# Writing the transposed K in another order, replacing a cross-partition maximum, and visiting later code first: one decode-attention kernel

## The chip, the cores and the metric

One core of a Trainium2 chip. The metric is the device time of one execution in microseconds (us). Some executions fall into a slower state (in experiment 1 two took 116.31 and 115.04 us at a mean granted clock of 0.87 and 0.85, against 113.21 and 112.99 us at 0.92 and 0.89), and these are left out of every comparison here. PE is the matmul engine, DVE the vector engine, ACT the scalar engine, POOL and SP the other two; SP only issues transfers here. The "granted clock" is the share of its full clock that PE was given. "Landing" is the moment at which a transfer has signalled its end.

## The reference, cut to what matters

```python
xn = layernorm(x)                                   # x: 2 x 1 x 448
q  = (xn @ wq)                                      # 16 query heads of 256
k, v = last 2048 rows of the caches, 8 kv heads, each for 2 query heads
s  = softmax(q k^T / 16) v @ wo
g  = silu(relu(xn @ w1) @ w2)
out = x + s * g
```

K and V of two batch entries and eight heads are 33.6 MB, and the weights bring the total to 44 MB. All of it is read once.

## The kernel before

Work goes in four units u = 0..3 (one batch entry, four heads each). T stands for the transposes of K, S for the score matmuls, PV for the matmuls of the softmax weights with V. The 2048 rows of a head are spread over 32 row groups r, and partition p of `kbuf` holds row group r and head h as p = 4 r + h. DVE transposes K in blocks of 32x32 (32-bit elements, each a pair of bf16 values), and PE multiplies the result with the queries. Four matmuls, one for each head, run side by side in four column strips of the array (in the trace of the kernel before one score matmul lasts 1.07 us, and eight of them take 1.97 to 2.00 us together).

```python
def do_T(u, blk):                       # DVE: 2048 elements of 32 bits per partition
    src = kbuf[u % 2][:, :].bitcast(F32).tensor
    dst = kt[blk][:, :].bitcast(F32).tensor
    ... e.transpose(view(dst, 0, [[1, 32 * NT]]), view(src, 32 * blk, [[DH // 2, NT], [1, 32]]))
        # waits for K of u and for the scores of u - 1 that read kt[blk]

def do_S(u, blk):                       # PE: eight matmuls
    for par in range(2):
        for i in range(4):              # head i
            ... mm(sbk[32 * i:32 * i + 8, :], qz[:, lo:lo + 8], view(kt[blk], 2 * i + par, [[64, NT], [8, 8]]), ...,
                   tile_position=(0, 32 * i))
```

A row of a transposed block holds its 32 columns in the order of the partitions, j = 4 r' + h (r' = 0..7). One head therefore takes every fourth 32-bit element: a step of 8 bf16 values, 16 bytes.

The softmax needs, for every score row, a bias that is the maximum over several partitions. Before, it goes through PE twice:

```python
rm   = max over the columns of sbk                       # DVE, 128 x 1
mbk  = transpose of rm by matmul with an identity         # PE
mrow = grouped max, negated, on one partition             # DVE
mall = mrow spread over 128 columns                       # DVE
mbk  = mall^T @ one                                       # PE: back to 128 partitions
bias = copy of mbk                                        # DVE
```

Transfers are issued from one queue in this order: wq (first part), K0, wq (rest), K1, V0, w1, w2; then K2 and V1 when T of u = 0 and the q matmuls are done; K3 after T of u = 1; V2 after PV of u = 0; V3 in two parts after PV of u = 1; wo in seven parts, shrinking in size, last. The end of the kernel is PV of u = 3, a few small steps, and 128 small matmuls with wo.

Of the kernel before, what the change touches and what calls it, by code (L numbers as in the profile page):

```python
# [22 lines left out]
class _Prog:  # L23
# [13 lines left out]
        self.lists[eng].append(o)  # L37
        return o

    def run(self, block):  # L40
        n = 0
        for ops in self.lists.values():
            for o in ops:
                for d in o.deps:
                    d.needed = True
        for e, ops in self.lists.items():
            sem, count = self.es.enter_context(self.nc.semaphore(f"s_{e}")), 0
            for o in ops:
                if o.dma:
                    n += 1  # L50
                    o.sem, o.value = self.es.enter_context(self.nc.semaphore(f"d_{n}")), 16
                elif o.needed:
                    count += 1
                    o.sem, o.value = sem, count

        def emit(eng, ops):
            seen = {}
            for o in ops:
                want = {}
                for d in o.deps:  # L60
                    if d.value > want.get(id(d.sem), (None, 0))[1]:
                        want[id(d.sem)] = (d.sem, d.value)
                for key, (sem, value) in want.items():
                    if value > seen.get(key, 0):
                        eng.wait_ge(sem, value)
                        seen[key] = value
                made = o.fn(eng) if o.fn else None
                if o.needed:
                    made.then_inc(o.sem, 16 if o.dma else 1)

        for name, e in (("gpsimd", POOL), ("sync", SP), ("scalar", ACTE), ("vector", DVE), ("tensor", PE)):
            def body(eng, ops=self.lists[e]):
                emit(eng, ops)
            getattr(block, name)(body)


def bass_recurrent_scan__sliding_block_cached__dense_activation_relu__decode_kernel(
# [27 lines left out]
    FC = DFF // 2  # L105
    WO_PARTS = [9, 7, 5, 4, 3, 2, 2]
    NWO = 16
    FIRST = 2
    NCOL = D // 4
    NROW = 4 * B  # L110
# [2 lines left out]
    with es:  # L113
        pr = _Prog(nc, es)

        def named(name, shape, dt):
            return es.enter_context(nc.sbuf_tensor(name, shape, dt))
# [4 lines left out]
        def view(t, off, dims, n=128, p0=0, pstep=1):  # L122
            width = t.shape[1]
            return bass.AP(t, p0 * width + off, [[width * pstep, n]] + dims)

        ident = named("ident", [128, 128], BF)
        ident_f = named("ident_f", [128, 128], F32)
        one_f = named("one_f", [128, 1], F32)
        par8 = named("par8", [128, 8], F32)
        par2 = named("par2", [128, 2], F32)  # L130
        qmask = named("qmask", [128, 8], F32)
# [23 lines left out]
        tmp = named("tmp", [NROW, NCOL], F32)  # L155
        out_sb = named("out_sb", [NROW, NCOL], BF)
        rm = named("rm", [128, 1], F32)
        mrow = named("mrow", [128, 8], F32)
        mall = named("mall", [128, 128], F32)
        bias = named("bias", [128, 1], F32)  # L160
        et = named("et", [128, 1024], BF)
        e_sb, e_t = et[:, 0:512], et[:, 512:1024]
# [44 lines left out]
        def load_v(u, cuts=(0, NT)):  # L207
# [15 lines left out]
        p_id = pr.op(POOL, lambda e: e.affine_select(  # L223
            out=ident[:, :], in_=ident[:, :], compare_op=ALU.not_equal, fill=1.0,
            base=0, pattern=[[-1, 128]], channel_multiplier=1), [i0])
        i1 = pr.op(POOL, lambda e: e.memset(ident_f[:, :], 0.0), [p_id])
        p_idf = pr.op(POOL, lambda e: e.affine_select(
            out=ident_f[:, :], in_=ident_f[:, :], compare_op=ALU.not_equal, fill=1.0,
            base=0, pattern=[[-1, 128]], channel_multiplier=1), [i1])
        p_one = pr.op(POOL, lambda e: e.memset(one_f[:, :], 1.0), [p_idf])  # L230
        p_z = [pr.op(POOL, lambda e, t=t: e.memset(t[:, :], 0.0)) for t in (mall, qrep, spread, h_z, at_z)][-1]

        a_z = [pr.op(ACTE, lambda e, t=t: e.memzero(t[:, :])) for t in (obk, sbk, hbk, obk_last)][-1]

# [7 lines left out]
        for e2 in range(2):  # L242
# [6 lines left out]
            out=par2[:, :], in_=view(ident, 0, [[1, 2], [2, 64]]), axis=AX.X, op=ALU.add), [p_id])  # L249
        v_par8 = pr.op(DVE, lambda e: e.tensor_copy(  # L250
            view(par8, 0, [[2, 4], [1, 2]]), view(par2, 0, [[0, 4], [1, 2]])), [v_par])
        v_qm = pr.op(DVE, lambda e: e.tensor_reduce(
            out=qmask[:, :], in_=view(ident, 0, [[16, 8], [1, 16]]), axis=AX.X, op=ALU.add))

# [34 lines left out]
        def do_T(u, blk):  # L289
            src = kbuf[u % 2][:, :].bitcast(F32).tensor  # L290
            dst = kt[blk][:, :].bitcast(F32).tensor
            st["T", u] = st["kt", u, blk] = pr.op(DVE, lambda e: e.transpose(  # L292
                view(dst, 0, [[1, 32 * NT]]), view(src, 32 * blk, [[DH // 2, NT], [1, 32]])),
                [d_k[u], st.get(("S", u - 1, blk))])

        def do_S(u, blk):
            b, v = divmod(u, 2)
            deps = [st["q"], st["kt", u, blk], st.get(("exp", u - 1)), a_z]
            for par in range(2):
                for i in range(4):  # L300
                    lo = 64 * (4 * i + 2 * v + b) + 8 * (2 * blk + par)
                    o = pr.op(PE, mm(sbk[32 * i:32 * i + 8, :], qz[:, lo:lo + 8], view(kt[blk], 2 * i + par, [[64, NT], [8, 8]]),
                                     blk == 0 and par == 0, blk == NBLK - 1 and par == 1, tile_position=(0, 32 * i)), deps)
                    deps = []
            st["S", u, blk] = o

        def softmax(u, fill=()):
            fill = list(fill)

            def meanwhile():  # L310
                if fill:
                    fill.pop(0)()

            meanwhile()
            v = pr.op(DVE, lambda e: e.tensor_reduce(out=rm[:, :], in_=sbk[:, :], axis=AX.X, op=ALU.max),  # L315
                      [st["S", u, NBLK - 1], st.get(("rmT", u - 1))])
            m = st["rmT", u] = pr.op(PE, lambda e: e.matmul(
                mbk_ap(0, 128, 1), lhsT=rm[:, :], rhs=ident_f[:, :], start=True, stop=True,
                is_transpose=True), [v, p_idf, st["mbk"]])
            v = pr.op(DVE, lambda e: e.tensor_reduce(  # L320
                out=view(mrow, 0, [[2, 4], [1, 2]], n=1), in_=view(mbk, 0, [[32, 4], [1, 2], [2, 4]], n=1), axis=AX.X, op=ALU.max, negate=True),
                [m])
            meanwhile()
            v = pr.op(DVE, lambda e: e.tensor_copy(  # L324
                view(mall, 0, [[32, 4], [2, 4], [1, 2]], n=1), view(mrow, 0, [[2, 4], [0, 4], [1, 2]], n=1)),
                [v, p_z, st.get(("bias", u - 1))])
            m = st["bias", u] = pr.op(PE, mm(mbk_ap(128, 1), mall[0:1, :], one_f[0:1, :], True, True), [v, p_one])
            v = st["mbk"] = pr.op(DVE, lambda e: e.tensor_copy(bias[:, :], mbk_ap(128, 1)),  # L328
                                  [m, st.get(("exp", u - 1))])
            meanwhile()  # L330
            a = st["exp", u] = pr.op(ACTE, lambda e: e.activation(  # L331
                e_sb, sbk[:, :], ACT.Exp, bias=bias[:, 0:1], accum_out=ssum[:, 0:1]),
                [v, st.get(("e_t", u - 1)), st.get(("gs", u - 1))])
            v = st["e_t", u] = pr.op(DVE, lambda e: e.transpose(e_t, e_sb), [a, st.get(("Pt", u - 1))])  # L334
            deps = [v, v_sp, st.get(("pt", u - 1))]
            for x in range(4):
                for g in range(4):
                    lo = 128 * (4 * x + g)
                    o = pr.op(PE, mm(view(pbk, 2 * x, [[8, 16], [1, 2]]), spread[:, lo:lo + 128],
                                     view(et, 512 + 2 * g, [[32, 16], [1, 2]]), g == 0, g == 3), deps)  # L340
                    deps = []
            st["Pt", u] = o
            v = st["pt", u] = pr.op(DVE, lambda e: e.tensor_tensor(  # L343
                out=view(pt[u % 2], 0, [[8, NT], [2, 4], [1, 2]]), in0=view(pbk, 0, [[2, NT], [0, 4], [1, 2]]),
                in1=view(hmask, 0, [[0, NT], [1, 4], [0, 2]]), op=ALU.mult), [o, v_hm, st.get(("PV", u - 2))])
            meanwhile()
            m = st["gs", u] = pr.op(PE, mm(mbk_ap(130, 1), gsum[:, :], ssum[:, 0:1], True, True), [v_gs, a, st["mbk"]])
            st["rs", u] = st["mbk"] = pr.op(DVE, lambda e: e.reciprocal(rs[:, u:u + 1], mbk_ap(130, 1)), [m])
            assert not fill
# [122 lines left out]
        softmax(0)  # L472
        scores(1)
        load_k(3)
        softmax(1, [fill(0, (0,)), fill(), fill(0, (1, 2)), fill(0, (3,))])
        attend_scale(0)
        do_H()
        do_F()
        load_v(2)
        scores(2)  # L480
        softmax(2, [fill(1, (0,)), fill(), fill(1, (1, 2)), fill(1, (3,))])
        attend_scale(1)
        load_v(3, (0, 48, 64))
        d_wo, j0 = {}, 0
# [2 lines left out]
            d_wo[j0] = pr.dma(SP, wo_sb[:, j0 * D:(j0 + n) * D], wo_src[v, :, j * D:(j + n) * D], [st["T", 2]])  # L487
            j0 += n
        scores(3)
        softmax(3, [fill(2, (0,)), fill(n=1), fill(2, (1, 2), 2), fill(2, (3,), 2)])  # L490
        attend_scale(2)
        idle_work(6)
        do_PV(3, (0, 1))
        attend_turn(2)
        do_PV(3, (2,))
# [20 lines left out]
        pr.op(ACTE, None, [d_o])  # L516

        with nc.Block() as block:
            pr.run(block)


# [26 lines left out]
```

## Time and profile before

| | before |
|---|---|
| time, median of 4 runs | 113.56 us (113.40 to 116.04; the last is a slow one, and the median of the other three is 113.44) |
| span of the profiled run | 112.5 us |
| data read | 44.1 MB, 392 GB/s over the span |
| K transposes on DVE | 16 x 2.28 us |
| eight score matmuls | 1.97 to 2.00 us |
| softmax bias, from end of the maximum to the exponential | 1.4 us |
| last landing of wo (issue plus time to landing) | 107.6 us |
| end of the last matmul | 110.3 us |

A row of the table of groups has: line of the kernel, engine, operation, output <- inputs, partitions x elements, count | busy us in all, mean ns of one | idle us of the engine ahead of it, and what ended most of it.

```profile
L274 PE MATMUL sbk<-kt,qz 128*8 128x512 bf16 x128 | 31.0, 1070 | 14.2 <-DVE kt L292 12.0
L292 DVE STREAM_TRANSPOSE kt<-kbuf 128x2048 f32<-128x2048 f32 x16 | 35.9, 2283 | 4.8 <-DMA kbuf<-in_A_k_cache_dram 4.8
...
L274 PE MATMUL obk<-vbuf,pt 128*16 128x512 bf16 x96 | 7.2, 402 | 0.0
L274 PE MATMUL obk<-kbuf,at_z 128*8 128x112 bf16 x128 | 6.6, 213 | 0.0
```

The score matmuls and the PV matmuls have the same number of columns and the same four strips, yet one score matmul takes 1070 ns and one PV matmul 402. The wo matmuls (last line) had no idle time ahead of them: when PE came to them, wo was there.

The chain of waits, in order of time (start us, us, what), for the stretch of u = 1 and for the end:

```profile
40.59 8.80 DVE kt L292 x4
...
49.43 2.00 PE sbk L274 x8
...
51.45 0.70 DVE rm L315
...
52.20 0.28 PE mbk L317
...
52.51 0.19 DVE mrow L320
...
52.72 0.18 DVE mall L324
...
52.95 0.39 PE mbk L274 x2
...
53.36 0.17 DVE bias L328
...
53.55 0.79 ACT et L331 x2
...
102.05 0.57 PE obk_last L274 x8
...
104.70 5.62 PE obk L274 x112
```

Four transposes take 8.80 us, 2.20 each, and only the last block of score matmuls (2.00 us) lies on the chain, since the others hide behind the next transpose. In u = 2 and u = 3 one more block of eight (1.97 us) lies on it.

The table of stretches (stretch, length, then busy us and count for PE, PE weight load, DVE, ACT, POOL; granted PE clock with 1.00 for full speed, share of the 16 transfer engines, GB/s):

```profile
85.00:90.00 5.00, 4.49 (x29) 0.50 (x21) 4.93 (x5) 0.00 (x0) 0.00 (x0) 0.57 0.98 416
90.00:95.00 5.00, 4.07 (x27) 0.56 (x20) 2.36 (x4) 0.00 (x0) 0.00 (x0) 1.00 0.98 418
...
105.00:110.00 5.00, 5.00 (x106) 5.00 (x104) 0.00 (x0) 0.00 (x0) 0.00 (x0) 1.00 0.18 63
```

The transfer engines are full to the end of the data, as in every stretch from 5 us on, and PE still works 2.7 us after the last landing.

### The profile page before, as it was taken

Reading aid. Unit: us, or ns where it says so; the run is one execution under the profiler, and the core shown is the slowest. Engines: PE = TensorE matmul, PEld = TensorE weight load, DVE = VectorE, ACT = ScalarE, POOL = GpSimd, SP = SyncE. Lnnn points to the kernel's source line nnn. Section 1 sums busy time; section 2 is a strip of 40 time slices with the busy share of each in tenths; the row PEclk is TensorE's granted clock in tenths of the full one; section 3 lists DMA queues with packets and bytes.
Section 4 is the critical chain, followed back from the end, with each engine's and each line's share of the span. In section 5 each row is a group of like instructions: output and inputs, shape, how many; then the busy total and the mean of one; then the engine's idle time right before and its main releaser. Section 6 shows DMA issues by size and latency. Waiting matters only on the chain.

```text
span 112.5 us, 1423 instructions
## 1 busy us (share of the span) xinstructions
PE 65.0 (58%) x621; PEld 22.8 (20%) x621; DVE 61.3 (55%) x86; ACT 9.7 (9%) x18; POOL 3.8 (3%) x14
## 2 busy tenths in 40 slices
PE   0010000371996227997786329887509887898992
PEld 0000000110110220002346301012301002343991
DVE  2067059987002489954452499924699944425001
ACT  4980000000000200000200000002000000200000
POOL 6700000000000000000000000000000000000000
PEclk9999999999599755599859965699965699999999
DMA  3989989989989989998999999999899999999600
GB/s 68 493 373 524 408 386 429 489 373 501 431 373 489 443 339 400 511 444 373 454 466 387 419 472 396 419 477 408 384 483 396 402 428 399 430 405 407 225 6 1
DMA packets 3050, 44.20 MB, mean 393 GB/s; under 512 B 354, under 2 KB 612, under 8 KB 1508
## 3 DMA queue, kind: packets, MB, share of 16 engines
q1 hardware_dynamic: 3008, 44.11, 92.6%
q8 instruction: 5, 0.08, 0.3%
q10 hardware_dynamic: 36, 0.01, 0.0%
q14 instruction: 1, 0.01, 0.0%
HBM read 44.11 MB, written 0.00 MB: 392 GB/s over the span
## 4 chain that ended last, share of the span: by engine, by line
PE 40%; DVE 35%; DMA 17%; ACT 3%; issue 2%; SPq 1%
DVE kt L292 20%; DMA vbuf<-in_A_wq_dram 17%; PE sbk L274 15%; PE obk L274 10%; PE mbk L274 3%; ACT et L331 3%; PE pbk L274 3%; PE fbk L274 3%; DVE et L334 3%; DVE rm L315 2%; PE obk_last L274 2%; PE wbk L274 2%; PE hbk L274 1%; DVE o_sb L368 1%; DVE qz L408 1%
## 5 line engine op out<-in xcount | busy, mean ns | idle before, releaser
L274 PE MATMUL sbk<-kt,qz 128*8 128x512 bf16 x128 | 31.0, 1070 | 14.2 <-DVE kt L292 12.0
L292 DVE STREAM_TRANSPOSE kt<-kbuf 128x2048 f32<-128x2048 f32 x16 | 35.9, 2283 | 4.8 <-DMA kbuf<-in_A_k_cache_dram 4.8
L274 PE MATMUL obk<-vbuf,xr 128*4 128x512 bf16 x28 | 3.1, 618 | 13.2 <-DMA vbuf<-in_A_wq_dram 13.2
L315 DVE TENSOR_REDUCE rm<-sbk 128x1 f32<-128x512 f32 x4 | 2.8, 692 | 13.7 <-PE sbk L274 13.7
L331 ACT ACTIVATE et<-sbk,bias 128x512 bf16<-128x512 f32 x4 | 2.7, 687 | 76.2 <-DVE bias L328 76.2
L274 PEld LDWEIGHTS sbk<-kt,qz 128*8 128x8 bf16 x128 | 2.1, 87 | 29.2 <-DVE kt L292 21.9
L274 PE MATMUL obk<-vbuf,pt 128*16 128x512 bf16 x96 | 7.2, 402 | 0.0
L274 PE MATMUL obk<-kbuf,at_z 128*8 128x112 bf16 x128 | 6.6, 213 | 0.0
L274 PEld LDWEIGHTS obk<-kbuf,at_z 128*8 128x8 bf16 x128 | 6.3, 87 | 0.0
L274 PE MATMUL mbk<-ident,xg 2*128 2x2 bf16 x7 | 0.3, 163 | 8.0 <-DVE xg L243 8.0
L274 PE MATMUL pbk<-et,spread 128*128 128x32 bf16 x64 | 2.6, 193 | 3.8 <-DVE et L334 3.8
L334 DVE STREAM_TRANSPOSE et<-et 128x512 bf16<-128x512 bf16 x4 | 2.8, 712 | 3.4 <-ACT et L331 3.4
L343 DVE TENSOR_TENSOR pt<-pbk,hmask 128x512 bf16<-128x512 f32 x4 | 2.8, 692 | 3.0 <-PE pbk L274 3.0
L274 PEld LDWEIGHTS obk<-vbuf,xr 128*4 128x4 bf16 x28 | 0.8, 114 | 14.7 <-issue 14.7
L274 PE MATMUL fbk<-wf,h_z 128*8 128x112 bf16 x56 | 2.9, 213 | 1.4 <-DVE h_z L423 1.4
L274 PE MATMUL wbk<-q_n,ident 128*128 128x512 bf16 x13 | 3.6, 381 | 0.0
L274 PEld LDWEIGHTS pbk<-et,spread 128*128 128x128 bf16 x64 | 2.2, 104 | 5.4 <-DVE et L334 5.4
L511 DVE TENSOR_TENSOR tmp<-obk,g_sb 8x112 f32<-8x112 f32 x1 | 0.3, 263 | 5.4 <-PE obk L274 5.4
L274 PEld LDWEIGHTS fbk<-wf,h_z 128*8 128x8 bf16 x56 | 2.8, 87 | 1.8 <-issue 1.8
L274 PEld LDWEIGHTS obk<-vbuf,pt 128*16 128x16 bf16 x96 | 2.0, 92 | 5.6 <-issue 4.7
L274 PE MATMUL mbk<-one_f,mall 1*128 1x1 f32 x8 | 1.5, 256 | 1.7 <-DVE mall L324 1.7
L382 DVE TENSOR_TENSOR at_exp<-mbk,qmask 128x128 bf16<-128x128 f32 x4 | 1.2, 292 | 2.1 <-PE mbk L274 2.0
(76 smaller groups left out, 45.4 us busy)
## 6 DMA issues: line engine op xcount, KB each, us to landing
kbuf<-in_A_k_cache_dram SPq DMA_DIRECT2D x4, 4096.0 KB, 29.2
vbuf<-in_A_v_cache_dram SPq DMA_DIRECT2D x3, 4096.0 KB, 37.8
wf<-in_B_w_dram SPq DMA_DIRECT2D x2, 1568.0 KB, 43.8
vbuf<-in_A_v_cache_dram SPq DMA_DIRECT2D x1, 3072.0 KB, 15.3
vbuf<-in_A_wq_dram SPq DMA_DIRECT2D x1, 2560.0 KB, 19.6
vbuf<-in_A_wq_dram SPq DMA_DIRECT2D x1, 1024.0 KB, 4.9
vbuf<-in_A_v_cache_dram SPq DMA_DIRECT2D x1, 1024.0 KB, 17.2
kbuf<-in_A_wo_dram SPq DMA_DIRECT2D x1, 1008.0 KB, 19.0
```

The source lines that it names most:

```text
L274: return lambda e: e.matmul(out_ap, lhsT=lhsT, rhs=rhs, start=start, stop=stop, skip_group_check=True, **kw)
L292: st["T", u] = st["kt", u, blk] = pr.op(DVE, lambda e: e.transpose(view(dst, 0, [[1, 32 * NT]]), view(src, 32 * blk, [[DH // 2, NT], [1, 3 ...
L315: v = pr.op(DVE, lambda e: e.tensor_reduce(out=rm[:, :], in_=sbk[:, :], axis=AX.X, op=ALU.max), [st["S", u, NBLK - 1], st.get(("rmT", u - ...
L331: a = st["exp", u] = pr.op(ACTE, lambda e: e.activation(e_sb, sbk[:, :], ACT.Exp, bias=bias[:, 0:1], accum_out=ssum[:, 0:1]), [v, st.get(( ...
L334: v = st["e_t", u] = pr.op(DVE, lambda e: e.transpose(e_t, e_sb), [a, st.get(("Pt", u - 1))])
L343: v = st["pt", u] = pr.op(DVE, lambda e: e.tensor_tensor(out=view(pt[u % 2], 0, [[8, NT], [2, 4], [1, 2]]), in0=view(pbk, 0, [[2, NT], [0, ...
L368: v = st["osb", u] = pr.op(DVE, lambda e: e.tensor_scalar(out=o_sb[:, :], in0=view(out_bank(u), 0, [[1, 512]]), scalar1=rs[:, u:u + 1], sc ...
L382: st["at", u] = st["mbk"] = pr.op(DVE, lambda e: e.tensor_tensor(out=view(at_exp, 0, [[16, 8], [8, 2], [1, 8]]), in0=view(mbk, 136, [[1, 8 ...
L408: st["q"] = pr.op(DVE, lambda e, r=r: e.tensor_tensor(out=view(qz, r, [[64, 16], [8, 8], [2, 4]]), in0=view(q_t, 256 * r, [[1, 16], [32, 8 ...
L511: v_t = pr.op(DVE, lambda e: e.tensor_tensor(out=tmp[:, :], in0=obk[0:NROW, 0:NCOL], in1=g_sb[:, :], op=ALU.mult), [m_o, st["g"]])
```

## The change

The intent: let the score matmuls read `kt` at a step of 4 bytes instead of 16, by having the transpose write each block in the order h, r' instead of r', h; find the bias on DVE alone; and have PE jump, before anything else, to two later places of its own program and back, so that their instructions are fetched early (the trace of the changed kernel has four instruction fetches of 16 KB before 17 us, that of the kernel before none). There are also more idle matmuls, whose result nobody reads, ahead of the last PV.

```diff
@@ do_T
-                view(dst, 0, [[1, 32 * NT]]), view(src, 32 * blk, [[DH // 2, NT], [1, 32]])),
+                view(dst, 0, [[32, NT], [1, 8], [8, 4]]), view(src, 32 * blk, [[DH // 2, NT], [1, 32]])),
@@ do_S
-  view(kt[blk], 2 * i + par, [[64, NT], [8, 8]])
+  view(kt[blk], 16 * i + par, [[64, NT], [2, 8]])
@@ softmax: mbk, mrow, mall, mbk, bias (two on PE, three on DVE) become
+            v = pr.op(DVE, lambda e: e.transpose(rmt[:, :], view(rm, 0, [[0, 32]])), [v])
+            v = pr.op(DVE, lambda e: e.tensor_tensor(out=m8[:, :], in0=rmt[:, 0:8], in1=nmask[:, :], op=ALU.add), [v])
+            v = pr.op(DVE, lambda e: e.tensor_reduce(out=bias[:, :], in_=m8[:, :], axis=AX.X, op=ALU.max, negate=True),
+                      [v, st.get(("exp", u - 1))])
@@ emitting the PE program, with VISITS = [285, 530] (places among its operations)
+            if stubs:
+                nc.br("visit_0", engines=[eng.engine])
+                ...
+                if i in stubs:
+                    nc.br(f"past_{k}", engines=[eng.engine])
+                    nc.switch_bb(f"visit_{k}", parent=top)
+                    eng.nop()
+                    nc.br(next visit, or back to the start)
@@ (cut: set-up of nmask, unused identity tiles removed, fills regrouped)
-        idle_work(6)
+        idle_work(10)
```

The write pattern `[[32, 64], [1, 8], [8, 4]]` puts four elements 32 bytes (8 elements) apart, then starts again 4 bytes further on.

More of the change, by code (lines that the diff above doesn't have):

```diff
@@ L38, in dma, with run @@
         return o
-    def run(self, block):
-        n = 0
+    def run(self, block, stubs):
+        n, nc = 0, self.nc
         for ops in self.lists.values():
@@ L54, in run, with emit @@
                     o.sem, o.value = sem, count
-        def emit(eng, ops):
+        def emit(eng, ops, stubs=()):
             seen = {}
-            for o in ops:
+            if stubs:
+                nc.br("visit_0", engines=[eng.engine])
+                top = nc.cur_bb.parent
+                nc.switch_bb("visit_end", parent=top)
+            for i, o in enumerate(ops):
+                if i in stubs:
+                    k = stubs.index(i)
+                    nc.br(f"past_{k}", engines=[eng.engine])
+                    nc.switch_bb(f"visit_{k}", parent=top)
+                    eng.nop()
+                    nc.br(f"visit_{k + 1}" if k + 1 < len(stubs) else "visit_end", engines=[eng.engine])
+                    nc.switch_bb(f"past_{k}", parent=top)
                 want = {}
@@ L71, in run, with body @@
         for name, e in (("gpsimd", POOL), ("sync", SP), ("scalar", ACTE), ("vector", DVE), ("tensor", PE)):
-            def body(eng, ops=self.lists[e]):
-                emit(eng, ops)
+            def body(eng, ops=self.lists[e], e=e):
+                emit(eng, ops, stubs if e == PE else ())
             getattr(block, name)(body)
@@ L107, in bass_recurrent_scan__sliding_block_cached__dense_activation_relu__decode_kernel @@
     NWO = 16
+    VISITS = [285, 530]
     FIRST = 2
@@ L126, in bass_recurrent_scan__sliding_block_cached__dense_activation_relu__decode_kernel @@
         ident = named("ident", [128, 128], BF)
-        ident_f = named("ident_f", [128, 128], F32)
-        one_f = named("one_f", [128, 1], F32)
         par8 = named("par8", [128, 8], F32)
@@ L157, in bass_recurrent_scan__sliding_block_cached__dense_activation_relu__decode_kernel @@
         rm = named("rm", [128, 1], F32)
-        mrow = named("mrow", [128, 8], F32)
-        mall = named("mall", [128, 128], F32)
+        nmask = named("nmask", [128, 8], F32)
+        rmt = named("rmt", [128, 32], F32)
+        m8 = named("m8", [128, 8], F32)
         bias = named("bias", [128, 1], F32)
@@ L225, in bass_recurrent_scan__sliding_block_cached__dense_activation_relu__decode_kernel @@
             base=0, pattern=[[-1, 128]], channel_multiplier=1), [i0])
-        i1 = pr.op(POOL, lambda e: e.memset(ident_f[:, :], 0.0), [p_id])
-        p_idf = pr.op(POOL, lambda e: e.affine_select(
-            out=ident_f[:, :], in_=ident_f[:, :], compare_op=ALU.not_equal, fill=1.0,
-            base=0, pattern=[[-1, 128]], channel_multiplier=1), [i1])
-        p_one = pr.op(POOL, lambda e: e.memset(one_f[:, :], 1.0), [p_idf])
-        p_z = [pr.op(POOL, lambda e, t=t: e.memset(t[:, :], 0.0)) for t in (mall, qrep, spread, h_z, at_z)][-1]
+        p_z = [pr.op(POOL, lambda e, t=t: e.memset(t[:, :], 0.0)) for t in (qrep, spread, h_z, at_z)][-1]
         a_z = [pr.op(ACTE, lambda e, t=t: e.memzero(t[:, :])) for t in (obk, sbk, hbk, obk_last)][-1]
@@ L251, in bass_recurrent_scan__sliding_block_cached__dense_activation_relu__decode_kernel @@
             view(par8, 0, [[2, 4], [1, 2]]), view(par2, 0, [[0, 4], [1, 2]])), [v_par])
+        v_nm = pr.op(DVE, lambda e: e.tensor_scalar(
+            out=nmask[:, :], in0=par8[:, :], scalar1=-1.0, scalar2=1e30, op0=ALU.add, op1=ALU.mult), [v_par8])
         v_qm = pr.op(DVE, lambda e: e.tensor_reduce(
@@ L301, in do_S @@
                     lo = 64 * (4 * i + 2 * v + b) + 8 * (2 * blk + par)
-                    o = pr.op(PE, mm(sbk[32 * i:32 * i + 8, :], qz[:, lo:lo + 8], view(kt[blk], 2 * i + par, [[64, NT], [8, 8]]),
+                    o = pr.op(PE, mm(sbk[32 * i:32 * i + 8, :], qz[:, lo:lo + 8], view(kt[blk], 16 * i + par, [[64, NT], [2, 8]]),
                                      blk == 0 and par == 0, blk == NBLK - 1 and par == 1, tile_position=(0, 32 * i)), deps)
@@ L315, in softmax @@
             v = pr.op(DVE, lambda e: e.tensor_reduce(out=rm[:, :], in_=sbk[:, :], axis=AX.X, op=ALU.max),
-                      [st["S", u, NBLK - 1], st.get(("rmT", u - 1))])
-            m = st["rmT", u] = pr.op(PE, lambda e: e.matmul(
-                mbk_ap(0, 128, 1), lhsT=rm[:, :], rhs=ident_f[:, :], start=True, stop=True,
-                is_transpose=True), [v, p_idf, st["mbk"]])
-            v = pr.op(DVE, lambda e: e.tensor_reduce(
-                out=view(mrow, 0, [[2, 4], [1, 2]], n=1), in_=view(mbk, 0, [[32, 4], [1, 2], [2, 4]], n=1), axis=AX.X, op=ALU.max, negate=True),
-                [m])
-            meanwhile()
-            v = pr.op(DVE, lambda e: e.tensor_copy(
-                view(mall, 0, [[32, 4], [2, 4], [1, 2]], n=1), view(mrow, 0, [[2, 4], [0, 4], [1, 2]], n=1)),
-                [v, p_z, st.get(("bias", u - 1))])
-            m = st["bias", u] = pr.op(PE, mm(mbk_ap(128, 1), mall[0:1, :], one_f[0:1, :], True, True), [v, p_one])
-            v = st["mbk"] = pr.op(DVE, lambda e: e.tensor_copy(bias[:, :], mbk_ap(128, 1)),
-                                  [m, st.get(("exp", u - 1))])
+                      [st["S", u, NBLK - 1]])
+            v = pr.op(DVE, lambda e: e.transpose(rmt[:, :], view(rm, 0, [[0, 32]])), [v])
+            v = pr.op(DVE, lambda e: e.tensor_tensor(out=m8[:, :], in0=rmt[:, 0:8], in1=nmask[:, :], op=ALU.add), [v])
+            v = pr.op(DVE, lambda e: e.tensor_reduce(out=bias[:, :], in_=m8[:, :], axis=AX.X, op=ALU.max, negate=True),
+                      [v, st.get(("exp", u - 1))])
             meanwhile()
@@ L474, in bass_recurrent_scan__sliding_block_cached__dense_activation_relu__decode_kernel @@
         load_k(3)
-        softmax(1, [fill(0, (0,)), fill(), fill(0, (1, 2)), fill(0, (3,))])
+        softmax(1, [fill(0, (0,)), fill(0, (1, 2)), fill(0, (3,))])
         attend_scale(0)
@@ L480, in bass_recurrent_scan__sliding_block_cached__dense_activation_relu__decode_kernel @@
         scores(2)
-        softmax(2, [fill(1, (0,)), fill(), fill(1, (1, 2)), fill(1, (3,))])
+        softmax(2, [fill(1, (0,)), fill(1, (1, 2)), fill(1, (3,))])
         attend_scale(1)
@@ L489, in bass_recurrent_scan__sliding_block_cached__dense_activation_relu__decode_kernel @@
         scores(3)
-        softmax(3, [fill(2, (0,)), fill(n=1), fill(2, (1, 2), 2), fill(2, (3,), 2)])
+        softmax(3, [fill(2, (0,)), fill(2, (1, 2), 2), fill(2, (3,), 2)])
         attend_scale(2)
-        idle_work(6)
+        idle_work(10)
         do_PV(3, (0, 1))
@@ L518, in bass_recurrent_scan__sliding_block_cached__dense_activation_relu__decode_kernel @@
         with nc.Block() as block:
-            pr.run(block)
+            pr.run(block, VISITS)
 _INS = ['A_x', 'A_k_cache', 'A_v_cache', 'A_wq', 'A_wo', 'B_x', 'B_w1', 'B_w2']
```

## The prediction

> **What bounds the kernel.** (1) Transfers: 44.2 MB; the table of stretches has the DMA share at 0.94 to 1.07, about 420 GB/s, in every 5 us from 5 to 105 us: nothing is issued too late. Issue time plus time to landing gives K2 59.6, K3 79.1, V2 88.9, the parts of V3 96.2 and 98.7, the seven parts of wo 101.2 to 107.6 us. (2) The chain of waits, compute from 21.5 us on: K transposes 20%, score matmuls 15%, then softmax pieces. The last PV ends at 102.6; the 128 wo matmuls run from 103.7 to 110.3 without a DMA wait (52 ns each), ending 2.7 us after wo's last landing. So the transfers let the last matmul come only about 2 us earlier.
>
> **What changes.**
> - Scores read kt at a step of 4 bytes, not 16. Eight score matmuls take 1.97 to 2.00 us at clock 0.5 and 1.0 alike, so the read sets them; eight PV matmuls of the same tiling, read contiguously, take 0.54 us. [...] Estimate: 0.55 (full clock) to 1.0 us (half) per eight. On the chain: the 32 of u=0 (7.4 us to about 3) and the last eight of u=1 to 3 (1.2 us each): about 8 us.
> - Bias: 1.4 us (two PE passes, three DVE ops) becomes three small DVE ops, estimated 0.5 us from this trace's 0.17 to 0.19 us ones. Four times 0.9: 3.5 us.
> - K transposes write each element 32 bytes from the last. Today 2.28 us for 2048 elements, 1.1 ns each. The copy into spread reads at 64-byte steps no slower (512 in 0.58 us); no such write is in the trace. I expect 2.25 to 2.35 us.
> - PE fetches later code early. The trace has five 16 KB instruction fetches, the last at 103 and 109 us, but the chain shows no fetch stall (issue gaps 0.02 to 0.14 us). Worth about 0.
> [...]
>
> **How much counts.** The compute gain of about 11 us is mostly absorbed: T of u=2 would wait for K2 (59.6; it starts at 64.7 now), T of u=3 for K3 (79.1; now 82.0); its softmax ends near 93.5, and PV of u=3 waits for V3 at 98.7. Then 0.55 us of PV, 1.1 us to the first wo matmul at 100.4; these follow the landings, the last rows at 107.6 plus a backlog of 0.7: last matmul near 108.3, not 110.3. Gain about 2 us.
>
> **Prediction: 111.7 us, 110.3 to 113.2. Faster by over 2%: 0.35; within 2%: 0.58; slower: 0.07.**
>
> **What would show it.** Eight score matmuls at 0.5 to 1.0 us; transposes near 2.28 us; DVE idle for K's transfers rising from 5 us to 10 or more; PV of u=3 and wo matmuls waiting on DMA; last wo landing still 107 to 108 us.
>
> **What would make it wrong.** A permuted write that costs the transposes 2x makes DVE the bound, over 118 us; up to about 1.4x the slack hides it. [...] If the end of the transfers moves, say because late instruction fetches held it up, the gain may pass 3 us.

Three passages are cut where the text marks it. About 8 us of scores and 3.5 us of bias make about 11 us, of which the transfers leave about 2 (last matmul at 108.3 instead of 110.3 us), and 113.56 less that was put at 111.7. That the score matmuls would take 0.55 to 1.0 us was the estimate: that a read at 4 bytes runs like the contiguous one of PV, where eight matmuls took 0.54 us at a granted clock of 1.00 (from 101.33 us in the trace of the kernel before) and 0.96 at 0.50 (from 55.71 us).

## The result, and the profile after

The changed kernel took 129.88 us (median of 4 runs, 129.43 to 130.41) against 113.56 us: a ratio of 1.144, with a 95% interval of 1.137 to 1.152. It is 14% slower. Ratios here and below are the mean time of one kernel's fast runs over that of the other's fast runs of the same rounds, so they are not quite the ratios of the medians quoted.

The groups that answer to those shown of before:

```profile
L300 DVE STREAM_TRANSPOSE kt<-kbuf 128x2048 f32<-128x2048 f32 x16 | 59.1, 3781 | 4.2 <-DMA kbuf<-in_A_k_cache_dram 4.2
L282 PE MATMUL sbk<-kt,qz 128*8 128x512 bf16 x128 | 15.9, 613 | 39.9 <-DVE kt L300 37.7
...
L282 PE MATMUL mbk<-ident,xg 2*128 2x2 bf16 x7 | 0.3, 160 | 12.2 <-issue 12.2
```

The K transposes went from 2283 to 3781 ns. The score matmuls became as fast as hoped, and PE now waits 37.7 us for the transposes instead of 12.0. The third line is PE's first work: it comes at 12.2 us, and what held it was not a wait but "issue".

The chain of waits in the stretch of u = 1:

```profile
43.63 14.60 DVE kt L300 x4
...
58.27 1.05 PE sbk L282 x8
...
59.35 0.70 DVE rm L323
...
60.08 0.22 DVE rmt L325
...
60.32 0.18 DVE m L326
...
60.52 0.17 DVE bias L327
...
60.72 0.79 ACT et L330 x2
```

The bias (0.67 us, from the end of the maximum at 60.05 to the exponential at 60.72) and the scores (1.05 us) shrank about as forecast. Four transposes take 14.60 us, 3.65 each, instead of 8.80. Sixteen times 1.45 us is 23.2 us more on DVE, which is on the chain nearly throughout.

The stretches:

```profile
85.00:90.00 5.00, 3.88 (x43) 1.36 (x44) 2.57 (x6) 0.78 (x2) 0.00 (x0) 0.50 0.34 144
90.00:95.00 5.00, 1.35 (x22) 0.61 (x18) 4.31 (x4) 0.00 (x0) 0.00 (x0) 0.84 0.47 167
...
110.00:115.00 5.00, 4.67 (x47) 2.18 (x40) 2.22 (x4) 0.34 (x2) 0.00 (x0) 0.89 0.38 146
```

The transfers now run dry near 90 us (a busy share of 0.34 and 0.47 in the first two rows, against 0.98 before): V3 may not be issued before PV of u = 1, and that is late. The bound has moved from the transfers to DVE.

### The profile page after: what moved, and what is told of

Same layout as the page of the kernel before. It is cut to its first block, busy times and chain, and to the rows that moved or that the text cites. A ratio compares the mean times of both kernels' runs of the same rounds, so it can differ in the third digit from the quotient of the medians.

```text
span 127.6 us, 1402 instructions
## 1 busy us (share of the span) xinstructions
PE 50.1 (39%) x610; PEld 22.2 (17%) x612; DVE 84.5 (66%) x87; ACT 9.7 (8%) x18; POOL 3.1 (2%) x10
## 4 chain that ended last, share of the span: by engine, by line
DVE 58%; PE 24%; DMA 13%; ACT 2%; issue 1%; SPq 0%
DVE kt L300 46%; DMA kbuf<-in_A_k_cache_dram 13%; PE obk L282 9%; PE sbk L282 5%; PE wbk L282 2%; PE pbk L282 2%; PE fbk L282 2%; ACT et L330 2%; DVE et L333 2%; DVE rm L323 2%; PE obk_last L282 2%; DVE o_sb L367 2%; PE mbk L282 1%; DVE qz L407 1%; DVE tmp L438 1%
## 5 line engine op out<-in xcount | busy, mean ns | idle before, releaser
L300 DVE STREAM_TRANSPOSE kt<-kbuf 128x2048 f32<-128x2048 f32 x16 | 59.1, 3781 | 4.2 <-DMA kbuf<-in_A_k_cache_dram 4.2
L282 PE MATMUL sbk<-kt,qz 128*8 128x512 bf16 x128 | 15.9, 613 | 39.9 <-DVE kt L300 37.7
L282 PE MATMUL obk<-vbuf,pt 128*16 128x512 bf16 x96 | 10.6, 589 | 0.0
L282 PE MATMUL mbk<-ident,xg 2*128 2x2 bf16 x7 | 0.3, 160 | 12.2 <-issue 12.2
L282 PEld LDWEIGHTS obk<-vbuf,pt 128*16 128x16 bf16 x96 | 2.9, 122 | 5.0 <-issue 4.8
L282 PE MATMUL pbk<-q_n,qrep 128*128 128x512 bf16 x1 | 0.6, 609 | 6.0 <-DVE q_n L402 6.0
```

Of the source, the lines that this page charges most:

```text
L282: return lambda e: e.matmul(out_ap, lhsT=lhsT, rhs=rhs, start=start, stop=stop, skip_group_check=True, **kw)
L300: st["T", u] = st["kt", u, blk] = pr.op(DVE, lambda e: e.transpose(view(dst, 0, [[32, NT], [1, 8], [8, 4]]), view(src, 32 * blk, [[DH // 2 ...
```

## The experiments

Theory A: the permuted write alone makes the kernel slow. Rival B: the visits or the new bias chain hold the kernel up. Two rivals say, within theory A, what in the pattern makes the write slow. Rival C: it costs by the run of the access pattern, whatever its bytes. Rival D: one particular step is slow. Where a text of an expectation is cut, the cut is marked in it. Twelve kernels ran. Numbers of a run's time are medians of all its runs; ratios are to the kernel before in the same rounds.

### 1. The changed kernel without the permutation

```diff
-view(dst, 0, [[32, NT], [1, 8], [8, 4]])      and  view(kt[blk], 16 * i + par, [[64, NT], [2, 8]])
+view(dst, 0, [[1, 32 * NT]])                  and  view(kt[blk], 2 * i + par, [[64, NT], [8, 8]])
```

> The changed kernel with the K transposes writing contiguously again and the scores reading at a 16-byte step again; the new bias and the visits stay. Theory A (the permuted write alone makes the kernel slow[...]): transposes back from 3.65 to 2.28 us, eight score matmuls back to 1.97 us, time 111 to 113.5 us. Rival B (the visits or the new bias chain hold the kernel up): transposes fast but time stays above 120 us. The visits may still delay the first landings (K of u=0 at 17.5 instead of 15.4 us).

Measured: the two fast runs took 113.21 and 112.99 us, ratio 0.995 (0.988 to 1.001). Transposes 2.28 us, eight score matmuls 1.97 us. The slowness is gone, so rival B falls. The first K transpose still started at 17.2 us.

### 2. The kernel before with the permutation alone

```diff
-view(dst, 0, [[1, 32 * NT]])                  and  view(kt[blk], 2 * i + par, [[64, NT], [8, 8]])
+view(dst, 0, [[32, NT], [1, 8], [8, 4]])      and  view(kt[blk], 16 * i + par, [[64, NT], [2, 8]])
```

> The kernel before with the permuted transpose write and the 4-byte score step alone. Theory A: transposes 3.65 us each, eight score matmuls 0.55 to 1.05 us, time 130 to 134 us (the changed kernel, plus the old bias chain of about 0.85 us four times, less what the visits cost). Rival B: transposes near 2.28 us and time near 112 us.

Measured: 134.48 us, ratio 1.180 (1.164 to 1.195); transposes of 3.78 us in duration, as in the changed kernel. The permutation alone is enough, and it costs more than the whole change, whose new bias wins some back. The time is half a microsecond above the expected range. In the trace, PV matmuls of the unit before, which stand in PE's program ahead of and behind the two passes of the old bias, lie on the chain three times (0.85 and 1.81 us each time); without the visits but with the new bias (experiment 4) such a run of 24 lies on it once (2.56 us).

### 3. The transposes written in eight ways

The steps, in 32-bit elements, of the eight write patterns; the read side is untouched, so most results are wrong.

```diff
+FORM = [[[1, 32 * NT]], [[32, NT], [1, 2], [2, 16]], [[32, NT], [1, 4], [4, 8]], [[32, NT], [1, 8], [8, 4]],
+        [[32, NT], [1, 16], [16, 2]], [[32, NT], [2, 8], [16, 2], [1, 2]], [[32, NT], [4, 4], [16, 2], [1, 4]], [[1, 32], [32, NT]]]
```

> Wrong results on purpose. The kernel before, where the transposes of u=0 and 2 write in the forms: contiguous; step 8 bytes (runs of 16 elements); step 16 bytes (runs of 8); step 32 bytes (runs of 4, as in the change); those of u=1 and 3: step 64 bytes (runs of 2); pairs of neighbours, 8 bytes together, then a 64-byte step; quads of neighbours, 16 bytes together, then a 64-byte step; step 128 bytes (one element per 32x32 block and row). Theory A[...]: 2.28 for contiguous, step 8 bytes, pairs and quads; 3.65 for steps of 16, 32, 64 and 128 bytes. Rival C (cost per run of the access pattern, 2.7 ns each by the 1.37 us over 512 runs): pairs 5.1 us, quads 3.7, step 8 bytes 2.6, step 16 bytes 3.0, step 64 bytes 5.1. Rival D[...]: 32 bytes slow, others differ without order.

Measured, one line of the kernel for each form in that order (duration in ns: shortest/median/longest of the two, then first and last start):

```profile
L297 DVE STREAM_TRANSPOSE kt<-kbuf x2: 2289/2300/2310, 15.3 to 72.3; 128x2048 f32<-128x2048 f32 x2
L298 DVE STREAM_TRANSPOSE kt<-kbuf x2: 2257/2262/2268, 17.5 to 74.6; 128x2048 f32<-128x2048 f32 x2
L299 DVE STREAM_TRANSPOSE kt<-kbuf x2: 3794/3807/3820, 19.7 to 77.1; 128x2048 f32<-128x2048 f32 x2
L300 DVE STREAM_TRANSPOSE kt<-kbuf x2: 3781/3871/3961, 23.4 to 80.8; 128x2048 f32<-128x2048 f32 x2
L301 DVE STREAM_TRANSPOSE kt<-kbuf x2: 3620/3622/3624, 43.0 to 92.9; 128x2048 f32<-128x2048 f32 x2
L302 DVE STREAM_TRANSPOSE kt<-kbuf x2: 2265/2270/2274, 46.5 to 96.3; 128x2048 f32<-128x2048 f32 x2
L303 DVE STREAM_TRANSPOSE kt<-kbuf x2: 2272/2286/2300, 48.7 to 99.0; 128x2048 f32<-128x2048 f32 x2
L304 DVE STREAM_TRANSPOSE kt<-kbuf x2: 3727/3729/3731, 50.8 to 101.2; 128x2048 f32<-128x2048 f32 x2
```

There are two prices and nothing between. Contiguous, a step of 8 bytes (L298), pairs with a 64-byte jump (L302) and quads (L303) cost 2.26 to 2.30 us. Steps of 16, 32, 64 and 128 bytes (L299, L300, L301, L304) cost 3.6 to 3.9. Where an element has a neighbour in the order of writing at most 8 bytes away, the write costs no more than a contiguous one; where every step is 16 bytes or more it takes 1.6 to 1.7 times as long, for every step from 16 to 128 bytes and whatever the length of the run. Rival C would have made pairs one of the slowest forms, and rival D would have singled out one step; both fall. What in the pattern sets the price is not shown: a cost set by the innermost step alone (2.26 to 2.30 us up to 8 bytes, 3.6 to 3.9 from 16 on) fits these eight forms, and no form was run to tell it from another rule. Either way, it is the permuted write that is slow.

This run, whose scores are wrong, still passed the comparison with the reference. The comparison is therefore blind to the order of K in this case, and the layouts of all kernels here rest on their index arithmetic.

### 4. The changed kernel without the visits

```diff
-    VISITS = [285, 530]
+    VISITS = []
```

> The changed kernel without the two visits. If the visits' early instruction fetches cost the start its 2 us (K of u=0 lands at 17.5 instead of 15.4, first matmul at 12.2 instead of 8.0): K lands near 15.4 again and the time falls by 1.5 to 2.2 us, to about 128. If the visits are free: within 0.5 us of 129.9. If they help: slower than 130.4.

Measured: 127.61 us, ratio 1.124 (1.115 to 1.134), 2.3 us faster than with the visits. The two were measured in different rounds, but the intervals of their ratios to the kernel before (1.115 to 1.134, and 1.137 to 1.152) do not meet: the visits did cost time. PE's first two groups of matmuls, first in the changed kernel, then without visits (start us, us, engine, line, what; in brackets the idle time ahead and what ended it):

```profile
12.18 0.32 PE L282 MATMUL mbk<-ident,xg 2*128 2x2 bf16 x7 [12.18 <-issue]
23.67 3.16 PE L282 MATMUL obk<-vbuf,xr 128*4 128x512 bf16 x28 [11.17 <-DMA vbuf<-in_A_wq_dram]
```

```profile
8.01 0.34 PE L282 MATMUL mbk<-ident,xg 2*128 2x2 bf16 x7 [8.01 <-DVE xg L249]
21.57 3.16 PE L282 MATMUL obk<-vbuf,xr 128*4 128x512 bf16 x28 [13.22 <-DMA vbuf<-in_A_wq_dram]
```

PE's own delay (8.0 to 12.2 us) is harmless: both kernels then wait 11 us and more for wq. What counts is that wq lands 2.1 us later, and K0 too (first transpose at 17.5 instead of 15.4 us).

### 5, 6 and 7. A permutation that keeps pairs together

The forms showed how to have both: write two heads next to each other, then jump. Head h and row group r' go to position 16 (h // 2) + 2 r' + h % 2, and one head is read at a step of two 32-bit elements, 8 bytes.

```diff
-view(dst, 0, [[32, NT], [1, 8], [8, 4]])
+view(dst, 0, [[32, NT], [2, 8], [16, 2], [1, 2]])
-view(kt[blk], 16 * i + par, [[64, NT], [2, 8]])
+view(kt[blk], 32 * (i // 2) + 2 * (i % 2) + par, [[64, NT], [4, 8]])
```

It was put into the changed kernel, into the changed kernel without visits, and alone into the kernel before.

> The changed kernel with another permutation of K: the transpose writes two neighbours (8 bytes) and then jumps 64 bytes, and the scores read at a step of 8 bytes. Theory A[...]: transposes 2.27 us and eight score matmuls 0.55 us at full and 1.05 us at half clock. Then the rest of the prediction can be tested, since this is the change with the cost it was given there: last matmul near 108.3 us, held by the landings of V3 and wo, and 111.7 us (110.7 to 112.7). [...] If no floor from the transfers exists: time near 105 us, since 8 us of score time and 3.5 us of bias time are gone.

(The times for the score matmuls were the estimate that the read, too, is as fast at a step of 8 bytes as at one of 4; no run had shown it then.)

> The same without the visits. The visits delayed the first landings by 2.1 us; if the transfers' end sets the time, this delay is absorbed and the time is within 0.5 us of the run with visits; if the chain from the first landing still sets it, 2 us faster than with visits, 109.5 to 110.

> The kernel before with the paired permutation alone (old bias chain, no visits). The chain loses about 8 us of score time; with the floor from the transfers the time is 111.5 to 112.5 us, nearly as fast as with the new bias too; without a floor near 105.5 us.

| kernel | median us | ratio to before | 95% interval |
|---|---|---|---|
| pairs, new bias, visits | 112.62 | 0.992 | 0.987 to 0.997 |
| pairs, new bias, no visits | 112.21 | 0.989 | 0.984 to 0.994 |
| pairs alone | 112.17 | 0.986 | 0.981 to 0.990 |

All three beat both the kernel before and the changed kernel, if only by about 1% against the kernel before. They are the change at nearly the cost that the prediction gave it (eight score matmuls take about 1.1 us instead of 0.55 to 1.0, see experiment 12), so they test the rest of the prediction. The version with new bias and without visits, groups, then waits (engine, line, waited for: us in all, times, longest), then the end of its chain:

```profile
L300 DVE STREAM_TRANSPOSE kt<-kbuf 128x2048 f32<-128x2048 f32 x16 | 35.9, 2284 | 9.9 <-DMA kbuf<-in_A_k_cache_dram 9.9
L282 PE MATMUL sbk<-kt,qz 128*8 128x512 bf16 x128 | 17.3, 644 | 27.0 <-DVE kt L300 24.9
```

```profile
DVE kt L300 <- DMA kbuf<-in_A_k_cache_dram: 9.9, 3, 4.7
PE obk L282 <- DMA kbuf<-in_A_wo_dram: 0.8, 1, 0.8
PE obk_last L282 <- DMA vbuf<-in_A_v_cache_dram: 0.4, 1, 0.4
```

```profile
75.38 25.60 DMA kbuf<-in_A_wo_dram
...
101.02 0.95 PE obk L282 x16
...
102.09 5.87 PE obk L282 x112
```

Transposes are back at 2.28 us. DVE waits three times for K (4.8 us before, 9.9 now), the last PV waits for V3, and the first wo matmul waits for wo to land at 101.0 us. The last matmul ends at 107.96 us, against the forecast 108.3. The transfers' end stands where it stood: the last part of wo lands at about 107.4 us (issue at 82.1 plus 25.3), against 107.6. The 2 us by which the visits delay the start is mostly absorbed (0.4 us between the first two medians, with overlapping intervals), and so is the new bias: with pairs in place it makes no visible difference. (The pairs alone show only the first of the waits for K and none for V3, but the same wait for wo.)

### 8. The kernel before with the visits alone

```diff
-            pr.run(block)
+            pr.run(block, VISITS)
```

(with the emitting code of the change)

> The kernel before with the two visits of the PE program alone. The visits delay the first landings by 2.1 us in every run that has them (K of u=0 at 17.4 instead of 15.4 us). In the kernel before compute runs without a gap from the landing of wq on, so the whole delay should come through: 115.0 to 116.0 us. If the early fetches save something later in the PE program: less than 115.

Measured: two fast runs, 116.87 and 116.49 us, ratio 1.024 (1.016 to 1.031); two more were slow. The first K transpose started at 18.4 us and the wq matmuls at 24.6, 3 us late. The time grew by 2.7 us, and both fast runs lie above the expected 115.0 to 116.0 us: nearly the whole delay comes through. No gain later in PE's program is seen.

### 9. The new bias alone

The changed kernel with neither permutation nor visits.

> The new bias chain alone (no permutation, no visits): the chain is 0.8 us shorter four times. Against the run with visits and without permutation (113.1 us in its fast runs), 2.1 us earlier at the start, but the transfers' floor near 112.2 us: 112.0 to 112.6 us.

Measured: 112.25 us, ratio 0.989 (0.981 to 0.997). The bias alone takes the kernel to the same floor as the pairs alone, or both: in the traces of all three the first wo matmul starts at 101.0 us and the last ends at 108.0. With the bias alone PE does not wait for the first part of wo; its own chain comes to it at that same moment.

### 10 and 11. One visit and four visits

```diff
-    VISITS = [285, 530]
+    VISITS = [530]                  # and, in the other, [160, 285, 410, 530]
```

> The changed kernel with one visit instead of two. [...] the first K transpose starts near 16.4 us, between 15.4 (none) and 17.5 (two). If any jump costs the same: 17.5 us. If only the number of 16 KB fetches before 16 us matters, the start follows that number (0 gives 15.4, 4 gives 17.4).

(The first idea was that each early 16 KB fetch delays the first landings by some time.)

> The changed kernel with four visits. By the first idea of the run with one visit: the first K transpose starts near 19 us if four visits bring more early fetches; if they bring the same four fetches, 17.5 us again.

| visits | 16 KB instruction fetches before 17 us | K0 lands | first K transpose | wq matmuls start |
|---|---|---|---|---|
| none | 0 | 15.4 | 15.4 | 21.57 |
| one | 2 | 16.6 | 16.6 | 22.75 |
| two | 4 | 17.5 | 17.5 | 23.67 |
| four | 3 (a fourth at 20 us) | 16.7 | 18.5 | 22.96 |

With four visits the first transpose did not wait for K0, which had landed at 16.7 us (issue at 1.2 plus 15.5). Ahead of the transposes in DVE's program stands a step that needs PE's first matmuls, and these came only at 17.4 us:

```profile
17.77 0.19 DVE L288 TENSOR_TENSOR xr<-mbk,par 128x28 bf16<-128x28 f32 x1 [7.71 <-PE mbk L282]
...
18.46 3.79 DVE L300 STREAM_TRANSPOSE kt<-kbuf 128x2048 f32<-128x2048 f32 x1
```

So more visits can also hold DVE up through PE's own delay, which was harmless in experiment 4. The landing of K0 follows the number of fetches before it, not the number of visits, at 0.4 to 0.6 us each (0.75 in experiment 8: four fetches, 3.0 us). For wq the number alone does not fix the delay: with four fetches before it, it was 1.4 us (four visits), 2.1 (two) and 3.0 (experiment 8). That each fetch delays the data is therefore supported, but its size is not settled. How a fetch holds up the data is not shown: the trace gives no view of a single transfer engine.

### 12. The score read at full clock

The pairs without visits, with idle matmuls ahead of every score block of u = 2 and 3 to keep PE at full clock (the granted clock was then 0.50 in the first of the eight blocks and 1.00 in the other seven; in the version with new bias, visits and pairs, without these idle matmuls, it was 0.50, 0.50 and 0.66 in three blocks looked at); u = 3 uses the 32-byte write and the 4-byte read of the change.

```diff
+                if u > 1:
+                    idle_work(8 if u == 2 else 14)
                 do_S(u, blk)
```

> The paired kernel without visits, with extra idle matmuls ahead of every block of score matmuls of u=2 and u=3 so that PE is at full clock there; u=2 writes pairs and reads at a step of 8 bytes, u=3 writes at a step of 32 bytes and reads at a step of 4. [...] eight of u=2 stay near 1.1 us at full clock, eight of u=3 fall to about 0.55 us. [...] Transposes of u=3 near 3.7 us each, of u=2 2.28 us.

The two outcomes set against each other: eight of u = 2 stay near 1.1 us at full clock while eight of u = 3 fall to about 0.55, or both take 0.55 us.

Measured: durations of one score matmul in the stretch of u = 2, then of u = 3.

```profile
L282 PE MATMUL sbk<-kt,qz x32: 629/642/654, 62.2 to 71.9; 128*8 128x512 bf16 x32
```

```profile
L282 PE MATMUL sbk<-kt,qz x32: 376/378/380, 83.0 to 94.4; 128*8 128x512 bf16 x32
```

The stretches of three blocks of eight (the granted clock is the third number from the end; counts are of instructions on `sbk` alone): the first two read at 8 bytes, the third at 4.

```profile
62.18:63.29 1.11, 1.11 (x8) 0.10 (x8) 0.00 (x0) 0.00 (x0) 0.50 0.89 384
65.68:66.79 1.11, 1.11 (x8) 0.10 (x8) 0.00 (x0) 0.00 (x0) 1.00 1.03 443
...
82.96:83.56 0.60, 0.60 (x8) 0.10 (x8) 0.00 (x0) 0.00 (x0) 1.00 1.14 492
```

At a step of 8 bytes, eight score matmuls take 1.11 us at clock 0.5 and at clock 1.0; at 4 bytes they take 0.60 us here at full clock (in u = 0 of the changed kernel 32 took 3.59 us, 0.90 for eight, though the clock granted there was 1.00 too); at 16 bytes, in the kernel before, 1.97. So the read by four matmuls side by side still gains from a step of 4 bytes over one of 8 (0.60 us against 1.11 at full clock), while the DVE write of experiment 3 costs the same in pairs as contiguous (2.27 and 2.30 us). The expectation in experiment 5, 0.55 us at full clock, was not met. In these kernels PE is mostly at half clock during the scores (0.50 in all twelve single blocks of u = 1 to 3 of the changed kernel), where eight matmuls at a step of 4 bytes take 1.02 to 1.05 us, so little is lost by the 8-byte step.

## Why the prediction was wrong, and where it was right

**Wrong: the cost of the permuted write.** The step that failed is "I expect 2.25 to 2.35 us" for the K transposes. They took 3.65 us from start to start (3.78 in duration). The argument was a DVE copy that *reads* at 64-byte steps as fast as the contiguous transposes, at 1.1 ns an element; it says nothing of a write, and the text itself noted that no such write was in the trace. In these two DVE instructions reads and writes differ: that copy reads at 64-byte steps at 1.1 ns an element (512 in 0.58 us), while the transposes that write at 64-byte steps take 1.8 ns (2048 in 3.62 us). The prediction costed the scatter in the read that the change improves (1.97 us for eight score matmuls against 0.54 for eight of PV), and did not ask what the same scatter costs in the write that it worsens. The change moves it from the matmul's read (eight from 1.97 to 1.05 us) to the transpose's write (2.28 to 3.78 us), so the engine that leads the chain gets the penalty. Experiments 1, 2 and 3 show that the permuted write alone does it; what in the write pattern sets its price is not shown.

**The size.** 23.2 us more on DVE; between the pairs and the permutation of the change, both without visits, the time moves from 112.21 to 127.61 us, 15.4 us. So about 8 us of the 23 were hidden, in a kernel whose DVE waited 9.9 us for K, and the rest came through. The forecast's warning put the write at 2x and above 118 us; it was 1.6x and 129.9. If about 8 us is all that can be hidden, the slack ends near 1.2x of the 35.9 us of transposes, not near the warning's 1.4x; this is an estimate, and no write between 1x and 1.6x was run.

**Wrong: the visits "worth about 0".** They cost 2.3 us in the changed kernel and 2.7 in the kernel before. The prediction looked for fetch stalls in the chain of waits and found none (gaps of 0.02 to 0.14 us). What it left out is that with early fetches wq and K0 land later, and everything waits for these. In kernels that reach the transfers' floor most of this is absorbed (0.4 us is left between the pairs with and without visits).

**Right: the scores and the bias.** Eight score matmuls at 4 bytes: forecast 0.55 to 1.0 us, measured 0.60 (experiment 12) and 0.90 (u = 0) at full and 1.05 at half clock. Bias: forecast 0.5 us instead of 1.4, measured 0.67.

**Right: the floor of the transfers.** The forecast absorbed nearly all of 11 us of compute gain in waits for K2, K3, V3 and wo, with the last matmul near 108.3 us. With the write repaired it ends at 107.96 us, the time is 112.2, and the two gains (pairs alone, bias alone) reach the same 112.2 us singly and together. The forecast 111.7 is 0.5 us low, as it subtracted the 2 us from the median of 113.56, while the profiled run that they had been read from took 114.34 us (114.3 less 2 is 112.3).

**Open.** How an early instruction fetch delays the data, and why the same number of fetches delayed wq by 1.4 to 3.0 us. Also what in the write pattern sets its price: the innermost step fits the eight forms, but no form was run to tell it from another rule.

## What to carry to other kernels

When a layout change removes a scattered access from one engine, look for the engine that inherits it, cost it from a duration of the same kind of access (a write for a write), and if the trace has none, measure it before trusting it. Look also for a layout in between: keeping pairs together took the penalty from the write (2.28 us again instead of 3.78) and still cut the read from 1.97 to 1.11 us. And find the floor of the transfers first; here what the forecast put at 11 us of shorter compute could buy 1.3 us.
